# Pooled attention and channel mixing: the two small attention products on quarters of TensorE

## The chip, the core and the metric

The kernel runs on one core of one Trainium2 chip. Its five engines work side by side: TensorE (PE in the profile, with PEld for its weight loads) multiplies matrices, VectorE (DVE), ScalarE (ACT) and GpSimd (POOL) do elementwise work, and SyncE (SP) issues DMAs. The metric is the device time of one execution in microseconds. Before the change it is 623.95 us, the median of three runs from 623.32 to 624.88. A measurement of this kernel can tell about 0.3% from no change.

## The reference

Eight batches, eight heads, 576 tokens, head dimension 64; everything is float32. Keys and values are averaged over groups of eight tokens, so that each head has 72 keys. The attention's output goes through a channel mixing step with a shift by one token.

```python
k_p = k.reshape(B, H, Sp, pool, D).mean(axis=3)          # Sp = 72, pool = 8
v_p = v.reshape(B, H, Sp, pool, D).mean(axis=3)
scores = scale * np.matmul(q, k_p.transpose(0, 1, 3, 2))
attn = np.exp(scores - max); attn = attn / (sum + 1e-09)
x = np.matmul(attn, v_p)                                 # then (B, S, H * D)

x_prev = x shifted by one token within a batch
xk = mu_k * x + (1.0 - mu_k) * x_prev
xr = mu_r * x + (1.0 - mu_r) * x_prev
k = np.maximum(xk @ w_k, 0.0)                            # w_k: 512 x 1024
v = k * k @ w_v                                          # w_v: 1024 x 512
r = 1.0 / (1.0 + np.exp(-(xr @ w_r)))                    # w_r: 512 x 512
out = r * v
```

## The kernel before

The 4608 tokens are cut into 36 tiles of 128 and 12 chunks of 384 tokens (three tiles each). A batch ends every 576 tokens, so four tiles hold tokens of two batches, and four chunks (1, 4, 7, 10) do.

**A tile** goes through `softmax` (line 680). Its scores are four matmuls, one for each pair of heads, at line 700: the queries of 128 tokens are the weights (128 rows: two heads of 64), and the keys of the pair stream by, in a buffer `kbd` in which the two heads' keys stand block by block on a diagonal, the rest zero. So half of the products are with zeros. A tile of two batches needs eight matmuls of 64 columns of weights. Then come the maximum, exponential, sum and reciprocal. The probabilities of 64 of the 72 keys are called the main part, those of the last 8 keys the remainder.

The product with the values needs the probabilities turned, keys by tokens. In chunks 0 and 1 PE turns them (`transposed`, line 815, `transposed_rest`, line 873). From chunk 2 on (`TURNED`) DVE turns blocks of 32 (`turned`, line 773), a DMA takes them to a buffer in DRAM, `passing`, and five DMAs bring a whole chunk back in another order into one buffer `turned_sb` (`fetch_turned`, line 800).

**Precision.** A float32 product can be taken whole, or from numbers that were split in a high and a low part of type fp32r, as three products (high by high, low by high, high by low). Chunk 0 is taken whole, all others are split, both in attention's second product and in the channel mixing. `split_turned` (line 845) splits the probabilities of a tile into `pth` and `ptl`, by an ACT cast and a DVE subtraction over 128 x 512, and makes a third form, `ptr`, for the remainder. The values stand on a diagonal as well: `vbd_h`, `vbd_l` (main) and `vbd_r` (remainder).

**A chunk** goes through `attended` (line 903), once for each pair of heads g = 0..3: four matmuls at line 940 (three main, one remainder; eight in a chunk with two batches) into one PSUM bank of three, then two ACT copies scaled by 1 - mu into `t`, a POOL copy of the token carried from the chunk before, and two DVE operations into `xm`, one for xk and one for xr. `x_parts` (line 978) splits each by an ACT cast and a POOL subtraction (`xkh`, `xkl`, `xrh`, `xrl`). Then `hidden` (line 988, matmuls at line 1011) makes eight tiles of k, each from the four column tiles (ct) of xk, which are the four pairs g; `gate` (line 1045, matmuls at 1063) makes r for three tiles; `mixed` (line 1074, matmuls at 1094) makes the output for three tiles.

**The order** of all instructions is made by a planner when the program is built (class `Order`, line 141). Each of these functions is a thread that says what it needs, what buffer it takes and how long its next step lasts on which engine; the planner gives an engine to the thread that can start first, and of those that could start within 0.1 us to the one with the smallest due time. A table `DUE` overrides due times by name, and other tables say which engine does a sum, a normalisation or a low part (`SUM_BY`, `NORM_BY`, `LOW_BY`, ...) and in which order the inputs are loaded at the start (`LOADS`). Each engine then runs its instructions strictly in the order that the planner wrote.

Of the kernel before, what the change touches and what calls it, by code (L numbers as in the profile page):

```python
# [17 lines left out]
P = 128  # L18
B, H, S, D = 8, 8, 576, 64
POOL = 8  # L20
# [1193 lines left out]
```

## Time and profile before

| | |
|---|---|
| median of the runs | 623.95 us |
| the profiled execution | 625.45 us |
| its span, first to last instruction | 623.6 us |
| mean granted clock of TensorE | 0.997 |
| instructions | 8940 |
| DMA | 68.61 MB, 110 GB/s on average |

The profile gives the busy time of each engine, the span in 40 slices, the chain of work that ended last (followed back from the last instruction, at each step to what released it), and groups of instructions by line. A row of a group reads: line, engine, operation, output <- inputs, shapes, count, then busy time in us and mean ns of one, then the idle time of the engine just before them and what ended it. On PE the mean ns of one matmul holds its way through the array too, and the next one starts earlier; what a stream of them costs is seen in the chain or in the rows in order of time, which show start, duration, line and count. A float32 matmul that isn't split is two records on PE and two weight loads on PEld.

### The profile page before, as it was taken

The numbers are of one execution on the slowest core, as the hardware profiler recorded it, in microseconds if no ns is written. First come the engines' busy times: TensorE is split into PE (matmuls) and PEld (weight loads), VectorE is DVE, ScalarE is ACT, GpSimd is POOL, SyncE is SP. The second block draws the span as 40 slices with busy tenths as digits, with TensorE's granted clock in tenths as the row PEclk, the third lists the DMA queues.
The fourth block names the chain that finished last, engine by engine and source line by source line (L and its number), as shares of the span: only waits on it lengthen the run. The fifth ranks groups of instructions, "written<-read, shape, count | busy, mean of one in ns | idle before, by whom it ended". The sixth has DMA issues, their size and how long they took to land.

```text
span 623.6 us, 8940 instructions
## 1 busy us (share of the span) xinstructions
PE 607.1 (97%) x3100; PEld 524.1 (84%) x3100; DVE 403.0 (65%) x826; ACT 363.7 (58%) x761; POOL 203.4 (33%) x292
## 2 busy tenths in 40 slices
PE   7789999999999999999999999999999999999997
PEld 6755457988988988988988988988988988988986
DVE  4789977975995844884884853794774753623511
ACT  4879975854575744774754753774654643633420
POOL 1130276326415215515614204713713313303100
PEclk9999999999899999999999999999999999999999
DMA  8997221562377132057147124049114013000001
GB/s 263 383 354 239 67 80 62 188 152 70 89 222 186 37 87 77 18 175 193 35 175 176 35 77 105 18 140 227 35 55 112 18 41 88 18 0 35 17 1 51
DMA packets 59453, 68.61 MB, mean 110 GB/s; under 512 B 11664, under 2 KB 43664, under 8 KB 59408
## 3 DMA queue, kind: packets, MB, share of 16 engines
q1 hardware_dynamic: 59264, 67.91, 36.6%
q8 instruction: 24, 0.39, 0.3%
q14 instruction: 21, 0.17, 0.1%
q10 hardware_dynamic: 144, 0.13, 0.1%
HBM read 49.75 MB, written 18.28 MB: 109 GB/s over the span
## 4 chain that ended last, share of the span: by engine, by line
PE 87%; DMA 5%; DVE 3%; POOL 2%; ACT 1%; issue 1%; SPq 0%; DVEq 0%; ACTq 0%; POOLq 0%
PE mm L1094 31%; PE mm L1011 29%; PE mm L1063 15%; PE bank L940 5%; PE sc L700 5%; DMA early_xrl<-in_vm 2%; DMA got_wk<-in_w_k 2%; DMA early_sl<-in_kT 1%; POOL xkl L984 1%; PE bank L448 1%; ACT t L946 1%; PE mm L591 1%; DVE xm L966 1%; POOL xrl L984 0%; ACT xkh L982 0%
## 5 line engine op out<-in xcount | busy, mean ns | idle before, releaser
L1011 PE MATMUL mm<-xkh,w_k 128*128 128x384 f32 x704 | 181.8, 339 | 1.5 <-ACT xkh L982 1.5
L1094 PE MATMUL mm<-w_v,sh 128*128 128x512 f32 x528 | 169.4, 391 | 0.0
L1011 PEld LDWEIGHTS mm<-xkh,w_k 128*128 128x128 f32 x704 | 127.1, 189 | 2.9 <-ACT xkh L982 1.7
L1011 PE MATMUL mm<-xkl,w_k 128*128 128x384 f32 x352 | 118.9, 338 | 1.7 <-POOL xkl L984 1.7
L1094 PEld LDWEIGHTS mm<-w_v,sh 128*128 128x128 f32 x528 | 99.2, 188 | 19.6
L1094 PE MATMUL mm<-w_v,sl 128*128 128x512 f32 x264 | 102.9, 390 | 0.0
L946 ACT ACTIVATE t<-bank,om_sb 128x384 f32<-128x384 f32 x96 | 49.8, 580 | 80.0 <-PE bank L940 78.7
L751 POOL TENSOR_TENSOR e<-e,sm 128x576 f32<-128x576 f32 x30 | 35.6, 1188 | 177.5 <-DVE sm L746 177.5
L1063 PE MATMUL mm<-w_r,xrh 128*128 128x512 f32 x264 | 84.2, 393 | 0.0
L1107 DVE TENSOR_TENSOR rs<-mm,rs 128x512 f32<-128x512 f32 (+1 forms) x37 | 24.9, 675 | 90.6 <-PE mm L1094 90.6
L966 DVE SCALAR_TENSOR_TENSOR xm<-bank,mu_sb,t 128x384 f32<-128x384 f32 x88 | 51.0, 611 | 36.9 <-POOL t L957 17.1
L1037 ACT CAST sh<-rk 128x384 fp32r<-128x384 f32 x88 | 44.8, 514 | 49.7 <-DVE rk L1031 49.4
L1011 PEld LDWEIGHTS mm<-xkl,w_k 128*128 128x128 f32 x352 | 66.6, 189 | 3.2 <-POOL xkl L984 3.2
L984 POOL TENSOR_TENSOR xkl<-xm,xkh 128x384 fp32r<-128x384 f32 x44 | 45.2, 1027 | 70.3 <-ACT xkh L982 70.1
L1039 DVE TENSOR_TENSOR sl<-rk,sh 128x384 fp32r<-128x384 f32 x88 | 51.8, 597 | 12.2 <-ACT sh L1037 10.5
L1063 PEld LDWEIGHTS mm<-w_r,xrh 128*128 128x128 f32 x264 | 49.6, 188 | 10.1
L1094 PEld LDWEIGHTS mm<-w_v,sl 128*128 128x128 f32 x264 | 49.6, 188 | 9.2
L1031 DVE SCALAR_TENSOR_TENSOR rk<-mm,rk 128x384 f32<-128x384 f32 x88 | 47.3, 548 | 11.1 <-ACT rk L1024 10.7
L1063 PE MATMUL mm<-w_r,xrl 128*128 128x512 f32 x132 | 51.4, 389 | 0.0
L1024 ACT ACTIVATE rk<-mm 128x384 f32<-128x384 f32 x88 | 42.2, 487 | 10.8 <-PE mm L1011 7.4
L984 POOL TENSOR_TENSOR xrl<-xm,xrh 128x384 fp32r<-128x384 f32 x44 | 45.6, 1036 | 3.3 <-ACT xrh L982 3.3
L580 POOL TENSOR_TENSOR stage<-stage 128x512 f32<-128x512 f32 (+5 forms) x51 | 45.0, 897 | 1.2
(126 smaller groups left out, 904.2 us busy)
## 6 DMA issues: line engine op xcount, KB each, us to landing
out<-rs SPq DMA_DIRECT2D x35, 256.0 KB, 2.0
passing<-pm SPq DMA_DIRECT2D x30, 288.0 KB, 2.2
qs<-in_qT SPq DMA_DIRECT2D x32, 256.0 KB, 3.6
stage<-in_kT SPq DMA_DIRECT2D x14, 576.0 KB, 4.7
turned_sb<-passing SPq DMA_DIRECT2D x40, 192.0 KB, 4.3
stage<-in_vm SPq DMA_DIRECT2D x14, 512.0 KB, 6.5
got_wk<-in_w_k SPq DMA_DIRECT2D x8, 512.0 KB, 9.0
got_wv<-in_w_v SPq DMA_DIRECT2D x8, 512.0 KB, 11.2
```

The lines of the kernel that those rows point to most:

```text
L580: nc_eng.tensor_tensor(out=st[:, :, :w], in0=st[:, :, :w], in1=st[:, :, w:2 * w], op=ALU.add)
L751: eng.tensor_tensor(out=e, in0=e, in1=sm.broadcast_to([P, 2, 4, KEYS]), op=ALU.mult)
L946: nc.scalar.activation(out=t[:, m, 1:n + 1], in_=xp, func=AF.Copy, scale=om_sb[:, m, g:g + 1])
L966: nc.vector.scalar_tensor_tensor(out=xm[:, :n], in0=xp, scalar=mu_sb[:, m, g:g + 1], in1=t[:, m, :n], op0=ALU.mult, op1=ALU.add,)
L984: nc.gpsimd.tensor_tensor(out=lo, in0=xm[:, :n], in1=hi, op=ALU.subtract)
L1011: nc.tensor.matmul(out=hp, lhsT=w[:, o], rhs=x[:, ct, o_t], start=(ct == 0 and k == 0), stop=(ct == NCT - 1 and k == len(terms) - 1),)
L1024: nc.scalar.activation(out=rk[:, :n], in_=hp, func=AF.Relu)
L1031: nc.vector.scalar_tensor_tensor(out=rk[:, :n], in0=hp, scalar=0.0, in1=rk[:, :n], op0=ALU.max, op1=ALU.mult)
L1037: nc.scalar.copy(out=sh, in_=rk[:, :n])
L1039: nc.vector.tensor_tensor(out=operand("sl", c)[:, jt, o_t], in0=rk[:, :n], in1=sh, op=ALU.subtract)
L1063: nc.tensor.matmul(out=bank, lhsT=x[:, ct, o], rhs=w, start=(ct == 0 and k == 0), stop=(ct == NCT - 1 and k == len(terms) - 1),)
L1094: nc.tensor.matmul(out=bank, lhsT=s[:, o], rhs=w, start=(jt == 0 and k == 0), stop=(jt == NJT - 1 and k == len(terms) - 1),)
```

## The change

Both small attention products are laid on quarters of TensorE: 64 rows (one head's dimension or keys) by 64 columns.

- **Scores** (line 664 of the changed kernel). For each pair of heads, two halves of the tile's tokens (columns) and two heads (rows) make four matmuls with 64 x 64 weights and 72 streamed columns, whole float32: 16 in a tile, whether it holds one batch or two. The two heads write to different banks. The keys stand in `ks` without zeros.
- **Second product** (`attended`, lines 870 and 885). One call now takes two pairs of heads (a = 0, 1) and two PSUM banks at once. First the remainders, as before, with fp32r and 128 columns; then for each batch four matmuls with 64 x 64 weights and up to 384 streamed columns, whole float32, on top of the remainders. What follows the matmuls (`t`, `xm`) is now a thread of its own, `shifted`, one for each bank.
- **Probabilities.** The main part isn't split any more. From chunk 2 on the matmuls read it where the DMA put it, in runs of 32 tokens. `split_turned` makes only `ptr`, once for a chunk. There are two buffers for the turned probabilities, `turned0` and `turned1`, given back after the chunk's second product; early on the second one also serves as room for inputs.
- **Values** stand in `vs` without zeros and unsplit. The buffers `kbd`, `vbd_h`, `vbd_l` and their clearing are gone; keys and values are copied by one ACT instruction and not two.
- The order of channels in `mu`, `w_k` and `w_r` is permuted on the host to suit.
- All the planner's tables and constants are new.

```diff
-LOADS = ("k0 k1 q0 wr3 q2 q1 r0 c0 q3 wk0 wv6 k2 wk1 q5 v1 wk4 wv1 k3 wr2 v0 wr0 wk3 q4 ...")
+LOADS = ("k0 k1 q0 wr3 q1 wv6 r0 c0 q2 q3 v1 wk1 wk4 k2 wk0 q5 k3 wv1 v0 wr2 wk6 wk2 v3 ...")
...
-    "keys 0 0": -9.94, "values 0 0": 24.5, "keys 0 1": -129.19, "values 0 1": -72.82,
+    "keys 0 0": 74.89, "values 0 0": -12.91, "keys 0 1": -160.77, "values 0 1": -59.65,
...
-    kbd = [const.tile([P, NPAIR, 2 * KEYS], F32, name=f"kbd{i}") for i in range(2)]
-    vbd_h = [const.tile([P, NPAIR, P], F32R, name=f"vbd_h{i}") for i in range(2)]
-    vbd_l = [const.tile([P, NPAIR, P], F32R, name=f"vbd_l{i}") for i in range(2)]
+    ks = [const.tile([P, NPAIR, KEYS], F32, name=f"ks{i}") for i in range(2)]
+    vs = [const.tile([P, NPAIR, D], F32, name=f"vs{i}") for i in range(2)]
...
-    turned_sb = const.tile([P, CH // BLOCK, 6 * BLOCK], F32, name="turned_sb")
+    turned_sb = [const.tile([P, CH // BLOCK, 6 * BLOCK], F32, name=f"turned{i}") for i in range(2)]
...
         for g in range(NPAIR):
-            k = (g % 2) * 2 * KEYS
-            for b, _, n, o in parts:
-                nc.tensor.matmul(
-                    out=halves[g // 2][o:o + n, 0, k:k + 2 * KEYS],
-                    lhsT=qs[:, g, o:o + n], rhs=kbd[b % 2][:, g, :], start=True, stop=True,
-                )
+            for o, b in sorted(owner.items()):
+                for h2 in range(2):
+                    r = slice(h2 * D, (h2 + 1) * D)
+                    nc.tensor.matmul(
+                        out=halves[h2][o:o + D, 0, g * KEYS:(g + 1) * KEYS],
+                        lhsT=qs[r, g, o:o + D], rhs=ks[b % 2][r, g, :], start=True, stop=True,
+                    )
...
-    def split_turned(i):
+    def split_turned(c):
...
-        nc.scalar.copy(out=pt_h, in_=main)
-        yield act(2 * P)
         nc.scalar.copy(out=ptr[:rows], in_=rest)
-        yield dve(NPAIR * P)
-        nc.vector.tensor_tensor(out=pt_l, in0=main, in1=pt_h, op=ALU.subtract)
...
-    def attended(c, g, p):
+    def attended(c, a, p):
...
-        bank = yield take("bank")
+        both = [(yield take("bank")), (yield take("bank"))]
...
-                terms = [(vh, ph), (vl, ph), (vh, pl)]
-            terms.append((vbd_r[i][:, r, 2 * j:2 * j + 2, :], operand("ptr", c)[:, r, o]))
-            for q, (v, pt) in enumerate(terms):
-                nc.tensor.matmul(
-                    out=xp[:, to], lhsT=v, rhs=pt, start=(q == 0), stop=(q == len(terms) - 1)
-                )
+        for q, (b, s, k, at) in enumerate(segs):
+            for h2 in range(2):
+                nc.tensor.matmul(
+                    out=both[h2][:, at:at + k], lhsT=vbd_r[b % 2][:, a, 2 * h2:2 * h2 + 2, :],
+                    rhs=operand("ptr", c)[:, a, off + at:off + at + k], start=(q == 0), stop=False,
+                    skip_group_check=True,
+                )
+        for q, (b, s, k, at) in enumerate(segs):
+            for j in range(2):
+                for h2 in range(2):
+                    r, to = slice(h2 * D, (h2 + 1) * D), both[h2][j * D:(j + 1) * D, at:at + k]
+                    if c >= TURNED:
+                        of = (off + at) // BLOCK
+                        pt = held["turned", c][r, of:of + k // BLOCK, (2 * a + j) * BLOCK:(2 * a + j + 1) * BLOCK]
+                        to = to.rearrange("p (a j) -> p a j", j=BLOCK)
+                    else:
+                        pt = operand("pt", c)[r, 2 * a + j, off + at:off + at + k]
+                    nc.tensor.matmul(
+                        out=to, lhsT=vs[b % 2][r, 2 * a + j, :], rhs=pt, start=False, stop=True,
+                        skip_group_check=True,
+                    )
...
+        for h2 in range(2):
+            order.add(att_due[c] + 2 * a + h2, shifted(c, 2 * a + h2, p, both[h2]))
```

What stands in order on PE, at three places. First the scores of a tile between the gate and the mixed products of chunk 2; before:

```order
L1063 MATMUL mm_119<-w_r_655,xrl_1208 128x512
L1063 MATMUL mm_119<-w_r_655,xrh_1207 128x512
L700 MATMUL sc_114<-kbd_70,qs_105 128x144 x4
L1094 MATMUL mm_120<-w_v_1042,sh_1333 128x512
L1094 MATMUL mm_120<-w_v_1042,sl_1373 128x512
```

and now:

```order
L1022 MATMUL mm_117<-w_r_752,xrl_1332 128x512
L1022 MATMUL mm_117<-w_r_752,xrh_1331 128x512
L664 MATMUL sc_112<-ks_70,qs_104 64x72 x16
L1053 MATMUL mm_118<-w_v_1101,sh_1393 128x512
L1053 MATMUL mm_118<-w_v_1101,sl_1450 128x512
```

The place is the same; four matmuls of 144 columns have become sixteen of 72.

Second, the product of chunk 5 between the mixed products of chunk 4, before (one pair of heads at each `L940` group, banks 117 and 115; a few mixed products between):

```order
L1094 MATMUL mm_119<-w_v_1013,sh_2171 128x512
L940 MATMUL bank_117<-pth_2121,vbd_h_72 128x384
L940 MATMUL bank_117<-pth_2121,vbd_l_74 128x384
L940 MATMUL bank_117<-ptl_2122,vbd_h_72 128x384
L940 MATMUL bank_117<-ptr_2123,vbd_r_76 128x384
L1094 MATMUL mm_120<-w_v_1042,sh_2171 128x512
L1094 MATMUL mm_120<-w_v_1042,sl_2211 128x512
L1094 MATMUL mm_120<-w_v_1042,sh_2171 128x512
L940 MATMUL bank_115<-pth_2121,vbd_h_72 128x384
L940 MATMUL bank_115<-pth_2121,vbd_l_74 128x384
L940 MATMUL bank_115<-ptl_2122,vbd_h_72 128x384
L940 MATMUL bank_115<-ptr_2123,vbd_r_76 128x384
```

and now, the second of its two calls:

```order
L1053 MATMUL mm_117<-w_v_1018,sh_2317 128x512
L870 MATMUL bank_115<-ptr_2222,vbd_r_74 128x384
L870 MATMUL bank_114<-ptr_2222,vbd_r_74 128x384
L885 MATMUL bank_115<-turned_98,vs_72 64x384
L885 MATMUL bank_114<-turned_98,vs_72 64x384
L885 MATMUL bank_115<-turned_98,vs_72 64x384
L885 MATMUL bank_114<-turned_98,vs_72 64x384
L1053 MATMUL mm_116<-w_v_1101,sh_2317 128x512
```

Eight matmuls of two pairs of heads have become two remainders and four quarters in one place. From chunk 3 on the two calls of a chunk stand behind the first and the second mixed tile of 24 matmuls, so that a whole mixed tile, and up to chunk 9 a tile's scores too, follow the second call ahead of `hidden`.

Third, the seam from the product of chunk 2 to `hidden` of chunk 2. Before, behind the last pair of heads:

```order
L940 MATMUL bank_116<-ptr_1030,vbd_r_76 128x384
L700 MATMUL sc_114<-kbd_69,qs_107 128x144 x4
L1011 MATMUL mm_120<-xkh_1198,w_k_477 128x384 x2
L1011 MATMUL mm_120<-xkl_1199,w_k_477 128x384
L1011 MATMUL mm_120<-xkh_1198,w_k_477 128x384 x2
L1011 MATMUL mm_120<-xkl_1199,w_k_477 128x384
L1011 MATMUL mm_118<-xkh_1198,w_k_643 128x384 x2
```

and now, behind the second call:

```order
L885 MATMUL bank_115<-turned_99,vs_72 64x384
L970 MATMUL mm_117<-xkh_1316,w_k_507 128x384 x2
L970 MATMUL mm_117<-xkl_1317,w_k_507 128x384
L970 MATMUL mm_117<-xkh_1316,w_k_507 128x384 x2
L970 MATMUL mm_117<-xkl_1317,w_k_507 128x384
L970 MATMUL mm_117<-xkh_1316,w_k_507 128x384 x2
L970 MATMUL mm_117<-xkl_1317,w_k_507 128x384
```

Each x2 and the row behind it are one column tile. Before, a tile's scores stood between, and after two column tiles the next bank's first ones followed; now the first bank's four column tiles follow at once, the third and fourth of which come from the call just ahead. The DMA queue of SP has 186 rows before and now, in another order.

More of the change, by code (lines that the diff above doesn't have):

```diff
@@ L370, in attention_then_channel_mix @@
     early = {}
-    for tag, n in (("sl", 2), ("ptl", 1), ("xrl", 1)):
-        t = sb.tile([P, n, 2 * POOL * KEYS], F32, name=f"early_{tag}", tag=tag)
-        for i in range(n):
+    places = [(tag, sb.tile([P, n, 2 * POOL * KEYS], F32, name=f"early_{tag}", tag=tag)) for tag, n in (("sl", 2), ("xrl", 1))]
+    places.append(("turned", turned_sb[1].rearrange("p a n -> p (a n)").rearrange("p (i n) -> p i n", i=2)))
+    for tag, t in places:
+        for i in range(t.shape[1]):
             got = t[:, i]
@@ L427, in constants @@
         order.make("ident")
-        for b in range(2):
-            yield "pool" if b else "dve", 0.6, False
-            (nc.gpsimd if b else nc.vector).memset(kbd[b], 0.0)
-            order.make(("kbd clear", b))
-        yield "dve", 0.5, False
-        nc.vector.memset(vbd_w, 0.0)
-        order.make(("values clear", 0))
-        for t in (vbd_h[1], vbd_l[1]):
-            yield "pool", 0.5, False
-            nc.gpsimd.memset(t.bitcast(F32), 0.0)
-        order.make(("values clear", 1))
     def warm():
@@ L609, in keys @@
     def keys(b, p):
-        yield need(("k", 2 * b + p), *([("scored", last_tile[b - 2])] if b > 1 else [("kbd clear", b)]))
+        yield need(("k", 2 * b + p), *([("scored", last_tile[b - 2])] if b > 1 else []))
         kind, raw, o = yield from sums(held.pop(("k", 2 * b + p)), KEYS, SUM_BY.get(f"k{2 * b + p}", "v"))
         gs = slice(2 * p, 2 * p + 2)
-        yield "act", 0.53, False
-        for h2 in range(2):
-            r = slice(h2 * D, (h2 + 1) * D)
-            nc.scalar.copy(out=kbd[b % 2][r, gs, h2 * KEYS:(h2 + 1) * KEYS], in_=o[r])
+        yield act(2 * KEYS)
+        nc.scalar.copy(out=ks[b % 2][:, gs], in_=o)
         done_with(kind, raw)
@@ L620, in values @@
     def values(b, p):
-        i = b % 2
-        as_is = b == 0 and whole(0, "p")
-        yield need(("v", 2 * b + p), ("attended", last_chunk[b - 2]) if b > 1 else ("values clear", b))
+        yield need(("v", 2 * b + p), *([("attended", last_chunk[b - 2])] if b > 1 else []))
         if not b:
@@ L626, in values @@
         kind, raw, o = yield from sums(held.pop(("v", 2 * b + p)), D, SUM_BY.get(f"v{2 * b + p}", "g"))
[L627 to L638 removed]
+        yield act(2 * D)
+        nc.scalar.copy(out=vs[b % 2][:, 2 * p:2 * p + 2], in_=o)
         done_with(kind, raw)
         order.make(("values", b, p))
[L641 to L652 removed]
     def last_values(b):
@@ L777, in turned @@
         yield "dve", 0.9, False
-        pairs = e.rearrange("p a (h two) k -> p (a h) two k", two=2)
         for h2 in range(2):
@@ L797, in free_turned, with free_second @@
         yield need(*[("full", kind, i) for kind, n in (("k", NJT), ("r", NCT), ("v", NJT)) for i in range(n)])
-        order.give("turned", turned_sb)
+        order.give("turned", turned_sb[0])
+    def free_second():
+        yield need(("early", "turned", 0), ("early", "turned", 1))
+        order.give("turned", turned_sb[1])
     def fetch_turned(c):
@@ L818, in transposed @@
         yield need(("pm", i), *([("attended", c - 1)] if c else []))
-        if not whole(c, "p"):
-            yield need(("early", "ptl", 0))
         got, pm = held.pop(("pm", i))
@@ L901, in transposed_rest @@
             order.make(("side", first + j))
-    def attended(c, g, p):
+    def attended(c, a, p):
         off, n = parts[c][p]
         segs = stretches(starts[c] + off, n)
-        as_is = whole(c, "p")
         mine = [i for i, t in enumerate(tiles) if t[0] == c and off <= t[1] < off + n]
-        yield need(*[(k, i) for i in mine for k in ("main", "side")])
-        yield need(
-            "om", *[("rest", b) for b, *_ in segs],
-            *[("values" if as_is else "value parts", b, q) for b, *_ in segs for q in range(2)],
-        )
+        if c >= TURNED:
+            yield need(("split", c))
+        else:
+            yield need(*[(k, i) for i in mine for k in ("main", "side")])
+        yield need("om", *[("rest", b) for b, *_ in segs], *[("values", b, a) for b, *_ in segs])
         if c:
@@ L917, in attended @@
             yield need(("early", "xrl", 0))
-        if g:
-            yield need(("attending", c, g - 1, p))
+        if a:
+            yield need(("attending", c, a - 1, p))
         if p:
-            yield need(("shifting", c, g, p - 1))
-        bank = yield take("bank")
+            yield need(*[("shifting", c, 2 * a + h2, p - 1) for h2 in range(2)])
+        both = [(yield take("bank")), (yield take("bank"))]
+        order.make(("attending", c, a, p))
+        yield "pe", SWITCH + sum(2 * pe(k)[1] + pe(k, True)[1] for _, _, k, _ in segs), False
@@ L923, in attended, with shifted @@
+        if c >= TURNED:
+            held["attended", c] = held.get(("attended", c), 0) + 1
+            if held["attended", c] == 2 * len(parts[c]):
+                order.give("turned", held.pop(("turned", c)))
+        order.count(("attended", c), 2 * len(parts[c]))
+        for h2 in range(2):
+            order.add(att_due[c] + 2 * a + h2, shifted(c, 2 * a + h2, p, both[h2]))
+    def shifted(c, g, p, bank):
+        off, n = parts[c][p]
+        segs = stretches(starts[c] + off, n)
         t = yield take("t")
-        order.make(("attending", c, g, p))
@@ L943, in attended @@
-        order.count(("attended", c), NPAIR * len(parts[c]))
         yield "act", 2 * (act(n)[1] + 0.05), False
```

154 lines of the change are left out of this document (53 added, 101 removed), and 112 rows, old and new, of the table DUE.

## The prediction

> **What bounds the kernel now.** First the page: busy times, slices, and the chain of work that ended last.
>
> ```profile
> PE 607.1 (97%) x3100; PEld 524.1 (84%) x3100; DVE 403.0 (65%) x826; ACT 363.7 (58%) x761; POOL 203.4 (33%) x292
> PE   7789999999999999999999999999999999999997
> PEclk9999999999899999999999999999999999999999
> GB/s 263 383 354 239 67 80 62 188 152 70 89 222 186 37 87 77 18 175 193 35 175 176 35 77 105 18 140 227 35 55 112 18 41 88 18 0 35 17 1 51
> PE 87%; DMA 5%; DVE 3%; POOL 2%; ACT 1%; issue 1%; SPq 0%; DVEq 0%; ACTq 0%; POOLq 0%
> ```
>
> PE is busy 97% of the span, carries 87% of the chain, and its clock is full in all slices but one. Work taken off PE is time; work taken off DVE (65%) or ACT (58%) is not. Busy durations overlap on PE, so I take costs from the chain over two chunks, where each piece is the time by which PE advances.
>
> ```profile
> 335.79 1.41 PE bank L940 x8
> 343.36 0.98 PE sc L700 x8
> 344.34 16.81 PE mm L1011 x96
> 362.13 8.20 PE mm L1063 x36
> 371.32 5.45 PE mm L1094 x24
> 383.14 1.77 PE bank L940 x16
> ```
>
> A whole float32 matmul is two records. One tile's scores (four matmuls, eight records) cost 0.98 us, 0.1225 each, and the next piece starts at 343.36 + 0.98 = 344.34: nothing is lost at the seam. The second product for two pairs of heads costs 1.41 (0.176 each), or 1.77 where a batch ends in the chunk (16 of 0.11). Hidden's matmuls take 16.81/96 = 0.175. The hidden, gate and mixed products are untouched.
>
> How often, from the groups by shape:
>
> ```profile
> L700 PE MATMUL sc<-kbd,qs 128*128 128x144 f32 x248 | 36.0, 288 | 1.8 <-ACT e L724 1.1 <-ACT kbd L616 0.6
> L700 PE MATMUL sc<-kbd,qs 128*64 128x144 f32 x64 | 4.8, 292 | 0.0
> L700 PE MATMUL mm<-kbd,qs 128*128 128x144 f32 x8 | 1.2, 299 | 1.7 <-DMA qs<-in_qT 1.7
> L940 PE MATMUL bank<-pth,vbd_h 128*128 128x192 f32 x32 | 9.8, 306 | 0.0
> L940 PE MATMUL bank<-pth,vbd_h 128*128 128x384 f32 x28 | 9.5, 339 | 0.0
> L940 PE MATMUL bank<-pth,rs 128*128 128x384 f32 x8 | 3.3, 499 | 0.6 <-ACT rs L631 0.6
> ```
>
> That is (248 + 8)/8 = 32 tiles of one batch, 64/16 = 4 tiles of two batches, 28/4 = 7 whole chunks, 32/8 = 4 divided ones (1, 4, 7, 10), and chunk 0.
>
> **What the trace shows of parts of TensorE.** The four two-batch tiles already use halves: 64 columns of weights, two outputs. The rows of PE in order of time around one of them, first in a wide and then in a very narrow window:
>
> ```profile
> 163.87 0.34 PE L1011 MATMUL mm<-xkl,w_k 128*128 128x384 f32 x1
> 164.14 1.20 PE L700 MATMUL sc<-kbd,qs 128*64 128x144 f32 x16
> 165.27 0.61 PE L1011 MATMUL mm<-xkh,w_k 128*128 128x384 f32 x2
> 165.71 0.34 PE L1011 MATMUL mm<-xkl,w_k 128*128 128x384 f32 x1
> ```
>
> ```profile
> 164.13 0.20 PEld L700 LDWEIGHTS sc<-kbd,qs 128*64 128x64 f32 x4 [0.25 <-issue]
> 164.14 0.34 PE L700 MATMUL sc<-kbd,qs 128*64 128x144 f32 x2
> ```
>
> Two matmuls start together and last 0.34 as a pair, so halves side by side do run at once: 16 records make eight slots of 0.1225. But the detour is not free. From 163.87 to 165.71 are 1.84 us, of which three whole matmuls are 0.525 and eight slots 0.98; **0.34 us is the price of going to parts and back** (rounded from 0.335).
>
> ```profile
> 55.84 5.81 PE mm L1011 x18
> L700 PEld LDWEIGHTS sc<-kbd,qs x312: 132/190/192, 8.7 to 504.1; 128*128 128x128 f32 x124, 128*64 128x64 f32 x32
> L591 PE MATMUL mm<-early_ptl,ident 128*128 128x144 f32 x16 | 2.2, 292 | 0.6 <-DMA early_ptl<-in_kT 0.6
> ```
>
> A whole float32 record of 384 columns takes 5.81/18 = 0.323, of 144 columns 0.1225: slots follow the columns streamed, so 72 columns should take 0.061. A weight load of 64 columns lasts 132 ns, of 128 columns 190; whole loads follow each other in 0.11 (the 192-column row above), so I put the floor for 64 at 0.11 - 0.058 = 0.052, under 0.061.
>
> **The change, part by part.**
>
> *Scores.* Sixteen quarter matmuls of 72 columns are 32 records, four at once: eight slots of 0.061 = 0.49, plus 0.34 for the detour = 0.83. A one-batch tile gains 0.98 - 0.83 = 0.15, times 32 = 4.8. A two-batch tile pays the detour already: 0.98 + 0.34 - 0.83 = 0.49, times 4 = 2.0.
>
> *Second product, for two pairs of heads.* Whole chunk: two remainder matmuls 0.35, two slots of 0.323 = 0.65, detour 0.34: 1.34 against 1.41, gain 0.07, times 14 = 1.0. Divided chunk: four of 0.11 = 0.44, four slots of 192 columns = 0.65, detour 0.34: 1.43 against 1.77, gain 0.34, times 8 = 2.7. Chunk 0: 4 x 0.323 + 2 x 0.176 = 1.64 against 1.34, times 2 = 0.6.
>
> Sum on PE: 4.8 + 2.0 + 1.0 + 2.7 + 0.6 = **11.1 us**. The uncertain price is the detour, paid 60 times (36 tiles, 24 products). Its ends: nothing (whole float32 next to whole matmuls, as at 343.36) and 0.45 (a third more, for four parts instead of two); the sum is then 31 or 4.5. I take 0.34, the only row of a detour. Reading probabilities in runs of 32 from DMA's buffer I price at nothing: the L591 sums stream two separate runs and last 292 against 288. Its other end, one more slot per product, would cost 24 x 0.32 = 7.7.
>
> *Off PE.* Splitting the probabilities goes (30 casts at 0.62 on ACT, as many subtractions on DVE), as do the zeroed buffers and half of the copies of keys and values. In steady chunks this lay beside PE: nothing. The remainder's split becomes three wide instructions per chunk, with a whole chunk's time before its product, since a second buffer lets DMA land early; the same 186 rows stand in the DMA queue.
>
> ```profile
> L857 ACT CAST pth<-turned_sb 128x512 fp32r<-128x512 f32 x30 | 17.5, 620 | 3.0 <-DMA turned_sb<-passing 3.0
> L946 ACT ACTIVATE t<-bank,om_sb 128x384 f32<-128x384 f32 x96 | 49.8, 580 | 80.0 <-PE bank L940 78.7
> L966 DVE SCALAR_TENSOR_TENSOR xm<-bank,mu_sb,t 128x384 f32<-128x384 f32 x88 | 51.0, 611 | 36.9 <-POOL t L957 17.1
> L982 ACT CAST xkh<-xm 128x384 fp32r<-128x384 f32 x44 | 22.6, 514 | 24.4 <-DVE xm L966 23.9
> L984 POOL TENSOR_TENSOR xkl<-xm,xkh 128x384 fp32r<-128x384 f32 x44 | 45.2, 1027 | 70.3 <-ACT xkh L982 70.1
> ```
>
> *The added wait.* A product now takes two of three banks at once. Behind it on PE stand mixed's matmuls. The second product needs one bank back from the first: two t's (1.16), two xm's (1.22) and a short POOL copy, about 2.6 us, under one 24-matmul mixed tile of 5.45. Hidden.
>
> *The seam to hidden.* After the second product, hidden's third column tile needs xkl of the third pair: four t's 2.32, cast 0.51, POOL 1.03, with latencies about 4.1 us; the fourth 5.1. In steady chunks a mixed tile (5.45), a tile's scores and two column tiles (1.05) stand between: covered. At chunk 2 only 1.05 does, so PE waits about 3.2 us. Before, that seam cost the following, along with a slowed clock, and two later seams also waited:
>
> ```profile
> PE mm L1011 <- POOL xkl L984: 1.7, 3, 0.7
> PE mm L1011 <- ACT xkh L982: 1.5, 1, 1.5
> 150.00:200.00 50.00, 48.06 (x248) 42.86 (x247) 39.16 (x84) 28.28 (x58) 21.81 (x29) 0.97 0.57 155
> 535.51 1.36 POOL xkl L984
> 580.21 1.01 POOL xkl L984
> ```
>
> 3.2 us of waiting is seen, some 2 of it at chunk 2 (the rest at the two last seams, where now a mixed tile covers). So chunk 2 loses 1.2 and the late seams win about 1.2: zero net. The clock (0.97 over 50 us, 1.5 us) I leave as it is.
>
> *Opening.*
>
> ```profile
> 11.92 7.18 DMA early_sl<-in_kT
> 19.12 11.09 DMA early_xrl<-in_vm
> 30.23 10.47 DMA got_wk<-in_w_k
> ```
>
> The first product waits for values that land at 30.23. One 512 KB weight block fewer now stands ahead of them: at 354 GB/s some 1.5 us. I count 1.0, with 3 either way, as every other load also moved.
>
> Sum: 11.1 + 1.0 = 12.1. The profiled execution took 625.45 us (span 623.6), 1.5 above the median of 623.95; 625.45 - 12.1 = 613.3, on the median's scale **611.9**.
>
> **Two rules of the Trainium skill, against the rows.** The pairs' slots keep 0.1225 though each needs a fresh load of 64 columns, so loads hide behind matmuls in the same rows. The Trainium skill, "TensorE: Matmul & The Clock Gate", Part 3 "The mechanism", says that a weight load overlaps running matmuls only where the row group differs. By that rule the slots there would be 0.1225 + 0.058; the trace disagrees.
>
> Sixteen matmuls of that tile start within 0.92 us, 0.057 apiece, by pairs at one moment. The same page of the Trainium skill, Part 1 "Wait — 56ns, not 53.3ns?", gives about 62 ns of sequencer time per matmul when hardware decoding is off. By that figure 32 records need 1.98 and the time would be an estimated 665.
>
> **Rivals.**
> - *Row halves take turns* (slower). Every pair in the trace splits columns; none splits rows. Then scores take 16 x 0.061 + 0.34 = 1.32, +0.34 x 32 = +10.9, two-batch tiles the same; products +0.65 each x 24 - 4.3 = +11.3. With -1.0: 645. It decides once a quarter slot exceeds (0.98 - 0.34)/8 = 0.08.
> - *The sequencer can't feed them* (slower). At 0.057 per record a tile takes 1.82 + 0.34 = 2.16: +1.18 x 32 + 0.84 x 4 - 4.3 - 1.0 = +36, 660. For it: no row shows more than 16 in 0.92; against: pairs start at once. It decides above 0.64/32 = 0.020 per record.
> - *Loads of two quarters follow each other* (slot 0.11): 1.22 per tile, +0.24 x 32 - 0.4 - 4.3 - 1.0 = +2: 626. The 0.1225 slots can't exclude it. Loads not hidden at all (slot 0.119): 1.29, +9.9 - 0.1 + 0.058 x 64 slots - 4.3 - 1.0 = +8: 632.
> - *A cheaper detour* (faster). Shorter slots may leave less to wait for at either seam: at 0.17, 60 x 0.17 = 10 more, 602.
>
> **Chances.** Forecast (604 to 619: opening, runs of 32, the seam) 0.64; cheaper detour 0.12; loads in turn 0.09, not hidden 0.02; row halves 0.07; sequencer 0.06. From 600 to 627 about 0.8 is held: the first three. Measurement separates 0.3%, 1.9 us: faster 0.78 (forecast, detour, a part of loads), within 0.05 (loads), slower 0.17.
>
> **What would show it.** In the chain, a tile's scores at 0.83 with 32 records, starts in fours; 1.3 means row halves or loads, 2 the sequencer. A pair of products at 1.34 and 1.43, the first whole matmul behind a detour late by a tenth or two. PE waiting once, some 3 us, at chunk 2, and hardly after. If PE shows waits on ACT or POOL at every chunk, the cover was misjudged; if values land after 30 us, the opening was.

## The result, and the profile after

| | before | after |
|---|---|---|
| median | 623.63 us (622.97 to 624.88) | 632.73 us (631.79 to 634.48) |
| ratio, 95% interval | | 1.0147 (1.0119 to 1.0174) |
| profiled execution, its span | 625.45 us, 623.6 us | 634.48 us, 632.7 us |
| mean granted clock | 0.997 | 0.985 |

The change made the kernel 9.1 us slower, where 12 us faster was forecast. First the page of the changed kernel: busy times, the granted clock in 40 slices, and the chain by engine.

```profile
PE 602.6 (95%) x4008; PEld 493.2 (78%) x4008; DVE 368.9 (58%) x743; ACT 328.1 (52%) x658; POOL 199.4 (32%) x286
PEclk9989999997999999999899999999999999999999
PE 80%; POOL 6%; DVE 4%; ACT 4%; DMA 3%; issue 2%; SPq 1%; DVEq 0%; POOLq 0%; ACTq 0%
```

Every engine has less to do than before, and PE's share of the chain fell from 87 to 80%: the end is now set, in places, by POOL, ACT and DVE. And the clock dips in four slices, where before it dipped in one. Now the chain of the changed kernel over one whole and the start of one divided chunk (start, us, engine, line, count).

```profile
318.28 0.66 PE sc L664 x32
318.94 8.38 PE mm L1022 x36
...
327.98 5.71 PE mm L1053 x24
333.69 0.35 PE bank L870 x2
334.04 0.81 PE bank L885 x8
334.85 5.66 PE mm L1053 x24
...
380.25 0.43 PE bank L870 x4
380.68 0.81 PE bank L885 x16
381.49 5.67 PE mm L1053 x24
```

For TensorE this is close to the forecast. A tile's 32 score records take 0.66 us and lengthen the piece behind them by 0.18 (8.38 against 8.20 before) or 0.26 (5.71 against 5.45): 0.84 to 0.92, against a forecast of 0.83. A pair of products takes 0.35 + 0.81 = 1.16 us plus 0.21 behind it (5.66 against 5.45), 1.37 against 1.34; in the divided chunk 0.43 + 0.81 + 0.22 = 1.46 against 1.43. So a quarter excursion costs up to 0.09 us more than forecast, an estimated 2 us over all 60, and most of the loss is elsewhere. The waits of the changed kernel, engine by engine (who, for whom: us in total, times, longest us), show where it is.

```profile
ACT vs L612 <- POOL stage L568: 24.5, 5, 6.2
...
PE mm L970 <- DVE rk L990: 12.0, 6, 2.9
...
PE mm L970 <- ACT xkh L941: 2.2, 1, 2.2
```

The same view of the kernel before has no row of PE for `rk` at all, and for the sums only this:

```profile
ACT vbd_h L631 <- POOL stage L580: 3.7, 2, 3.2
```

So the 12.0 us are new; 11.3 of them fall in chunks 4, 5, 7 and 8 and 0.7 in chunk 1. One of the four chunks, at the start of chunk 5's hidden, in order of time:

```profile
297.61 8.04 POOL L568 TENSOR_TENSOR stage<-stage 128x512 f32<-128x512 f32 x9
302.70 0.72 ACT L612 COPY vs<-stage 128x128 f32<-128x128 f32 x2 [6.24 <-POOL stage L568]
303.15 0.34 PE L970 MATMUL mm<-xkl,w_k 128*128 128x384 f32 x1
...
304.88 0.49 ACT L983 ACTIVATE rk<-mm 128x384 f32<-128x384 f32 x1
305.41 0.56 DVE L990 SCALAR_TENSOR_TENSOR rk<-mm,rk 128x384 f32<-128x384 f32 x1
306.02 0.56 PE L970 MATMUL mm<-xkh,w_k 128*128 128x384 f32 x1 [2.52 <-DVE rk L990]
```

POOL sums the values of a later batch, nine additions in 8.04 us. ACT stands for 6.24 us before the copy of these sums; behind it in its queue are an exponential, a cast and then the first relu of hidden (`rk`, 304.88), whose input, the twelve matmuls of hidden's first tile of k that began at about 297, was ready soon after 299. (The expectations of e2, e3 and e5 call these eight tiles of k hidden's column tiles.) DVE finishes it at 305.97. PE has three banks `mm`, has filled them with three tiles of k by 303.4, and needs the first one back: it stands for 2.52 us. The same is seen in chunks 4, 7 and 8, the chunks behind which the values of batches 4, 6 and 7 are summed. Behind some of these waits the clock drops, and behind two waits for x in chunks 0 and 2 as well, as the windows show (start:end, length, busy us of the five engines with counts, granted clock, DMA share, GB/s):

```profile
30.00:37.00 7.00, 4.86 (x23) 1.91 (x22) 4.78 (x10) 2.92 (x6) 2.05 (x5) 0.76 1.07 376
145.00:160.00 15.00, 12.63 (x57) 11.03 (x56) 5.08 (x9) 7.44 (x16) 12.50 (x16) 0.77 0.34 71
303.00:310.00 7.00, 4.47 (x17) 4.16 (x16) 5.23 (x13) 4.48 (x11) 3.60 (x5) 0.76 0.73 236
451.00:460.00 9.00, 6.13 (x26) 5.81 (x26) 6.33 (x16) 5.51 (x12) 4.49 (x7) 0.81 0.08 33
```

A mean of 0.76 over 7 us is 3.4 us at half speed (7 x 0.24 x 2). The four places hold 3.4, 6.9, 3.4 and 3.4 us, 17.1 in all, half of it lost: 8.5 us. Before there was one such place, in chunk 2 (0.76 over the 7 us from 155, again 3.4 us at half speed, 1.7 lost).

With the forecast's own -11.1 on PE and -1.0 in the opening, +12.0 at `rk` and +6.8 by the clock make +6.7; the last matmul begins 6.6 us later than before (625.9 against 619.4). The two forecast terms in this sum are not measurements, so the agreement is in part luck. The profiled span is longer by 9.1: the last DMA issue on ACT took 2.62 us there and 0.37 before. It took 0.37 again in e1, whose PE order is the same, and 2.14 in e3, so it goes with the execution and not with the change.

### The profile page after: what moved, and what is told of

Same layout as the page of the kernel before. It is cut to its first block, busy times and chain, and to the rows that moved or that the text cites. A ratio compares the mean times of both kernels' runs of the same rounds, so it can differ in the third digit from the quotient of the medians.

```text
span 632.7 us, 10535 instructions
## 1 busy us (share of the span) xinstructions
PE 602.6 (95%) x4008; PEld 493.2 (78%) x4008; DVE 368.9 (58%) x743; ACT 328.1 (52%) x658; POOL 199.4 (32%) x286
## 4 chain that ended last, share of the span: by engine, by line
PE 80%; POOL 6%; DVE 4%; ACT 4%; DMA 3%; issue 2%; SPq 1%; DVEq 0%; POOLq 0%; ACTq 0%
PE mm L970 28%; PE mm L1053 27%; PE mm L1022 16%; POOL stage L568 4%; PE bank L885 3%; PE sc L664 3%; ACT t L905 2%; DMA early_xrl<-in_kT 2%; DMA stage<-in_vr 1%; PE bank L870 1%; POOL xrl L943 1%; DVE stage L568 1%; DVE xm L925 1%; PE mm L579 1%; ACT xkh L941 0%
## 5 line engine op out<-in xcount | busy, mean ns | idle before, releaser
L970 PE MATMUL mm<-xkh,w_k 128*128 128x384 f32 x704 | 185.4, 345 | 14.2 <-DVE rk L990 12.0
L1053 PE MATMUL mm<-w_v,sh 128*128 128x512 f32 x528 | 171.4, 396 | 0.0
L970 PEld LDWEIGHTS mm<-xkh,w_k 128*128 128x128 f32 x704 | 129.8, 193 | 18.3 <-DVE rk L990 13.7
L970 PE MATMUL mm<-xkl,w_k 128*128 128x384 f32 x352 | 120.5, 342 | 0.2 <-POOL xkl L943 0.2
L715 POOL TENSOR_TENSOR e<-e,sm 128x576 f32<-128x576 f32 x29 | 34.1, 1175 | 187.6 <-DVE sm L710 181.3
L905 ACT ACTIVATE t<-bank,om_sb 128x384 f32<-128x384 f32 x96 | 48.2, 584 | 65.7 <-PE bank L885 65.7
L970 PEld LDWEIGHTS mm<-xkl,w_k 128*128 128x128 f32 x352 | 67.9, 193 | 0.9 <-POOL xkl L943 0.9
L990 DVE SCALAR_TENSOR_TENSOR rk<-mm,rk 128x384 f32<-128x384 f32 x88 | 48.6, 552 | 23.3 <-ACT rk L983 23.0
L943 POOL TENSOR_TENSOR xrl<-xm,xrh 128x384 fp32r<-128x384 f32 x44 | 47.5, 1087 | 5.6 <-ACT xrh L941 5.6
L1066 DVE TENSOR_TENSOR rs<-mm,rs 128x512 f32<-128x512 f32 (+1 forms) x37 | 24.7, 670 | 40.7 <-PE mm L1053 40.6
L568 POOL TENSOR_TENSOR stage<-stage 128x512 f32<-128x512 f32 (+5 forms) x48 | 41.6, 889 | 1.3
```

The costliest lines, as they stand in the source:

```text
L568: nc_eng.tensor_tensor(out=st[:, :, :w], in0=st[:, :, :w], in1=st[:, :, w:2 * w], op=ALU.add)
L715: eng.tensor_tensor(out=e, in0=e, in1=sm.broadcast_to([P, 2, 4, KEYS]), op=ALU.mult)
L905: nc.scalar.activation(out=t[:, m, 1:n + 1], in_=xp, func=AF.Copy, scale=om_sb[:, m, g:g + 1])
L943: nc.gpsimd.tensor_tensor(out=lo, in0=xm[:, :n], in1=hi, op=ALU.subtract)
L970: nc.tensor.matmul(out=hp, lhsT=w[:, o], rhs=x[:, ct, o_t], start=(ct == 0 and k == 0), stop=(ct == NCT - 1 and k == len(terms) - 1),)
L990: nc.vector.scalar_tensor_tensor(out=rk[:, :n], in0=hp, scalar=0.0, in1=rk[:, :n], op0=ALU.max, op1=ALU.mult)
```

## The experiments

Behind them is one table, made from PE's rows in order of time: when the first gate matmul of a chunk starts, against the kernel before, in us. It compares one profiled execution of each run; that of the kernel before took 625.45 us, 1.7 to 2.0 above its medians beside the runs (623.47 to 623.77), and those of the changed kernel and of e5 lie 1.8 and 3.0 above their own, so the last column is not the difference of the medians.

| run | median | chunk 0 | 2 | 3 | 5 | 8 | 11 | last matmul |
|---|---|---|---|---|---|---|---|---|
| changed kernel | 632.73 | -1.6 | -2.4 | -0.8 | +4.1 | +10.6 | +6.6 | +6.6 |
| e5, copies and casts later | 620.28 | -0.8 | -1.2 | +0.5 | +0.3 | +1.0 | -2.2 | -2.2 |
| e8, plan mended | 622.93 | -0.8 | +4.8 | +6.0 | +3.7 | +0.2 | -3.0 | -3.0 |
| e9, mended from chunk 3 | 616.92 | -1.9 | -4.1 | +0.6 | -1.8 | -5.3 | -8.5 | -8.5 |
| e10, and seams filled | 615.86 | -2.8 | -5.0 | -0.3 | -2.7 | -6.2 | -9.4 | -9.4 |
| e7, kernel before with new scores | 621.55 | -1.3 | -1.3 | -1.6 | -2.2 | -3.2 | -3.6 | -3.6 |

### Without the copy, and with the copy later (e1, e2): a miss

In e1 the last addition of a sum gets `vs` as its output (the change inside `sums` is left out here); in e2 only a need is added.

```diff
@@ values (e1) @@
-    kind, raw, o = yield from sums(held.pop(("v", 2 * b + p)), D, SUM_BY.get(f"v{2 * b + p}", "g"))
-    yield act(2 * D)
-    nc.scalar.copy(out=vs[b % 2][:, 2 * p:2 * p + 2], in_=o)
+    to = vs[b % 2][:, 2 * p:2 * p + 2]
+    kind, raw, o = yield from sums(held.pop(("v", 2 * b + p)), D, SUM_BY.get(f"v{2 * b + p}", "g"), to if b >= 4 else None)
+    if o is not None:
+        yield act(2 * D)
+        nc.scalar.copy(out=to, in_=o)
@@ values (e2) @@
+    if b >= 4:
+        yield need(("hid", last_chunk[b - 2], 3, 0))
     yield act(2 * D)
     nc.scalar.copy(out=vs[b % 2][:, 2 * p:2 * p + 2], in_=o)
```

> The changed kernel, but for batches 4 to 7 POOL's last addition of each value sum writes straight into vs, so that ACT has no copy of values there; the order of PE's matmuls is the same. Theory (ACT waits 6 us in that copy for POOL's sums, with hidden's first two relu's queued behind it, so that PE waits 2.5 us for a bank in chunks 4, 5, 7 and 8): PE's waits for DVE's rk fall from 12.0 us to under 2, ACT's waits for POOL's sums at that line from 24.5 to under 3, the clock keeps full speed at 306 and 456 us, and the time is 615 to 619 us against 632.7. Rival A (POOL's value sums delay the low parts xkl, or the quarters themselves cost it, and ACT's copy only stands beside): the waits turn into waits for xkl or others, time 628 or more. Rival B (waits go, but the lost time is elsewhere): 624 to 628.

> The changed kernel with all its work, but for batches 4 to 7 ACT's copy of the values is ordered only after hidden's fourth column tile has been issued; the order of PE's matmuls is the same. Theory (only the place of the copy in ACT's order costs the time): within 2 us of the run without the copy, 615 to 620 us, PE's waits for rk under 2 us. Rival (the copy's own work on ACT, or POOL's burst of sums, is what costs): 628 or more.

Measured: 633.01 us (ratio to the kernel before 1.0164, 1.0139 to 1.0188) and 633.46 us (1.0166, 1.0137 to 1.0195). Nothing was won: both theories failed. The waits of e1 and then of e2:

```profile
ACT vq L630 <- POOL stage L568: 19.7, 4, 5.3
...
PE mm L977 <- DVE rk L997: 12.4, 5, 4.1
...
ACT vs L619 <- POOL stage L568: 0.4, 1, 0.4
```

```profile
ACT vq L625 <- POOL stage L568: 19.1, 4, 5.0
...
PE mm L972 <- DVE rk L992: 10.9, 5, 4.1
...
ACT vs L614 <- POOL stage L568: 0.9, 1, 0.9
```

The copies' own wait is gone (24.5 to 0.4 and 0.9), and the next instruction of ACT that needs POOL's sums has taken it over: the cast of the remainder values `vq`, which needs all nine additions and stands behind the first relu and ahead of the second. PE stands as long as before, for the second bank and not the first. By these two runs alone the theory could have been given up; the row of `vq` says it was only too narrow.

### Both later (e5)

```diff
@@ values: as in e2; last_values: @@
+    if b >= 4:
+        yield need(("hid", last_chunk[b - 2], 5, 0))
     vq = yield take("vq")
```

> The changed kernel with all its work; for batches 4 to 7 both the copies of the values (after hidden's fourth column tile) and the cast of the remainder values vq (after its sixth) are ordered later on ACT. The run with the copies alone moved still waited, 12 us at rk, now 5.2 us on ACT in front of the cast of vq, which needs all nine of POOL's sums. Theory (any ACT instruction that needs these sums and stands ahead of hidden's relu's costs the same wait; together they are the loss): PE's waits for rk under 2 us, no half clock behind chunk 3, time 614 to 620 us. Rival A (a third consumer takes the wait over, DVE's steps on the values or the products of the next chunk but one): 626 or more. Rival B (the loss is in the quarters' neighbours): 626 or more, without waits on PE.

Measured: 620.28 us, ratio 0.9952 (0.9935 to 0.9970): 12.4 us less than the changed kernel, by the place of three instructions per batch in ACT's order; one place for a tile's scores moved too, from chunk 4 to chunk 9. The granted clock is full from chunk 3 on. The waits, and two rows of DVE in chunk 4:

```profile
PE mm L974 <- DVE rk L994: 5.6, 5, 1.7
...
ACT vs L614 <- POOL stage L568: 0.4, 1, 0.4
```

```profile
259.62 0.77 DVE L747 STREAM_TRANSPOSE pm<-e 128x256 f32<-128x256 f32 x2 [4.05 <-POOL e L719]
...
260.88 0.55 DVE L994 SCALAR_TENSOR_TENSOR rk<-mm,rk 128x384 f32<-128x384 f32 x1
```

What is left, 5.6 us, is mostly a third form of the same (0.7 of it is again the wait in chunk 1, which no edit touched): POOL normalises a tile's probabilities behind its nine additions, DVE waits 4.05 us for them with its transposes, and `rk` stands behind these in DVE's queue. That is rival A in small; the theory's figure for `rk` (under 2) was missed, its time by 0.3.

### The clock (e3)

```diff
+    if jt == 3 and ct == 0 and c in (4, 5, 7, 8):
+        unused = min(order.slots["bank"], key=lambda h: h[0])[1]
+        for _ in range(10):
+            nc.tensor.matmul(out=unused[:, :P], lhsT=ident, rhs=ident, start=True, stop=True)
```

> The changed kernel with ten matmuls of the identity by itself (128 columns, whole float32, about 2.2 us in all, into a bank that nobody reads) put on PE ahead of hidden's fourth column tile in chunks 4, 5, 7 and 8, where it waits 2.3 to 3.05 us; ACT's order stays. Theory (idle PE of over some 2.4 us costs a stretch of half clock behind it, 3.4 us long in two of the four chunks): the half-speed stretches at 306 and 456 us vanish and the time falls by 3 to 4 us, to 629 to 630; the waits in sum with the filling stay 10 to 12 us. Rival (the half-speed stretches come by themselves or follow something else): no change or up to 2 us slower, 632 to 635.

Measured: 629.75 us, 3.0 less than the changed kernel, ratio 1.0107 (1.0088 to 1.0126). Its windows:

```profile
300.00:315.00 15.00, 14.70 (x92) 14.51 (x91) 10.92 (x26) 7.63 (x17) 5.93 (x9) 1.00 0.55 168
450.00:465.00 15.00, 14.36 (x115) 13.67 (x114) 11.24 (x25) 9.12 (x20) 3.27 (x4) 1.00 0.37 80
```

The two stretches of half clock behind the waits are gone, with the waits still there, only filled with work for nobody. So two of the waits for `rk` cost 1.7 us each more than themselves. The theory's limit of some 2.4 us doesn't hold: waits of 2.09 and 2.19 us were followed by half clock too. The last section shows what decides.

### The sums planned as if they took no time, in the kernel before (e4)

```diff
-    yield (dve if eng == "v" else pool)(2 * n * cols)
+    yield ("pool", 0.0, True) if early else (dve if eng == "v" else pool)(2 * n * cols)
```

(`early` is set for the value sums of batches 4 to 7.)

> The kernel before the change, with one thing of the changed kernel's order: for batches 4 to 7 the planner counts POOL's value sums as taking no time, so that ACT's casts of the values stand ahead of hidden's first or second relu; the order of PE's matmuls and all the work are unchanged. Theory (this order alone costs the time, whatever TensorE's parts do): PE waits for rk at four chunks, 8 to 12 us in all, with one or two stretches of half clock: 632 to 639 us against 623.6. Rival (the order is harmless without the quarters): 623 to 625.

Measured: 648.48 us, ratio 1.0403 (1.0383 to 1.0423), 24.7 us slower: more than expected, and by another path. The edit moved more than ACT's casts. POOL's own order changed, and the waits are for x and not for `rk`; its waits, and POOL, ACT and POOL again in chunk 4:

```profile
PE mm L1011 <- ACT xkh L982: 14.6, 5, 3.9
```

```profile
247.25 5.97 POOL L580 TENSOR_TENSOR stage<-stage 128x512 f32<-128x512 f32 x7
253.17 0.19 POOL L953 COPY t<-carry 128x2 f32<-128x2 f32 x1
254.32 0.51 ACT L982 CAST xkh<-xm 128x384 fp32r<-128x384 f32 x1 [4.22 <-DVE xm L966]
```

The copy of one token, 0.19 us of work, stood behind seven additions, and the last quarter of x with it. The clock has its share: four stretches, 20.5 us at half speed, against one of 3.4 before. So this run doesn't show what it was made for, and the kernel before with ACT's casts alone earlier wasn't tried. It shows that in the kernel before, too, without any quarters, a misjudged place of POOL's sums costs 24.7 us with PE's matmuls in the same order.

### The scores alone (e7)

```diff
-    for b, _, n, o in parts:
-        nc.tensor.matmul(out=halves[g // 2][o:o + n, 0, k:k + 2 * KEYS], lhsT=qs[:, g, o:o + n], rhs=kbd[b % 2][:, g, :])
+    for o, b in sorted(owner.items()):
+        for h2 in range(2):
+            nc.tensor.matmul(out=halves[h2][o:o + D, 0, g * KEYS:(g + 1) * KEYS], lhsT=qs[r, g, o:o + D],
+                             rhs=kbd[b % 2][r, g, h2 * KEYS:(h2 + 1) * KEYS])
...
```

> The kernel before the change with the scores alone on quarters of TensorE (32 records a tile, and the order of heads in e, pm and px that goes with it; keys still read from the zero-padded buffer); the planner's costs are not touched, so every engine keeps its order. Theory (quarters are a plain gain of 0.15 us per one-batch tile and 0.49 per two-batch tile wherever the order is undisturbed): 6.8 us less than 623.8, 616 to 618 us, with no new waits. Rival (shorter scores only move the waits elsewhere, for the engines beside PE have no room): 621 to 624.

Measured: 621.55 us, ratio 0.9969 (0.9959 to 0.9979), a gain of 2.0 where 6.8 was expected. Its chain in steady chunks:

```profile
358.67 0.66 PE sc L702 x32
359.33 8.38 PE mm L1065 x36
...
368.38 5.71 PE mm L1096 x24
```

PE's order is the same as before but for the scores, so the two traces can be laid side by side matmul by matmul. A tile of one batch gains 0.14 to 0.15 us, as forecast, where hidden follows it, but only 0.12 to 0.13 where the gate follows and 0.07 to 0.08 where mixed follows: 0.34 for the three tiles of a chunk where 0.45 was forecast. The two tiles of two batches behind chunk 3 gain 0.47 each (0.49 forecast) and lose it at once, for x isn't ready earlier: in chunks 5 and 8 PE now waits 0.43 and 0.42 us for `xkl`, where before it didn't.

```profile
PE mm L1013 <- POOL xkl L986: 2.0, 4, 0.7
```

That is how the table comes to -3.6 at chunk 9 from -1.6 at chunk 3, 2.0 where the forecast's prices give 3.4. At chunk 2 the gain stands still; PE waits 2.9 us there for `xkh`, against 1.5 before. So the scores win on their own, but less than was forecast, and a tuned order gives part of it back at its tight seams. Theory and rival each hold in part; the time is the rival's.

### The plan (e8, e9)

Why did the copies come to stand there? Each follow-up of a second product, `shifted`, is a thread of its own in the changed kernel. In the kernel before it was the same thread as the product, and so was planned after it. The new thread asks only for a buffer `t`: nothing tells the planner that the product must be done. In the planner's own times the `t` of chunk 5's second product start at 268.3 and the product ends at 272.4 us. On the chip nothing can go wrong by that, since the engines' semaphores hold; but the plan believes that x and POOL's sums are ready 4 us early, and writes ACT's queue accordingly.

```diff
@@ attended, behind the matmuls @@
+    order.make(("product", c, a, p))
@@ shifted, ahead of its first step (in e9 for c >= 3 only) @@
+    yield need(("product", c, g // 2, p))
```

> The changed kernel with one line more in its planner: the thread that follows a second product (shifted) is planned no earlier than the end of that product's matmuls, as it was in the kernel before, where both were one thread. In the changed kernel's plan the t of the second product of chunk 5 starts at 268.3 and the product itself ends at 272.4, so x's low parts and POOL's value sums are planned some 4 us too early. Work is the same; every engine's order is planned anew (chunks 0 to 2 most). Theory (this lost need is why ACT's copies stand ahead of the relu's): in chunks 4, 5, 7 and 8 the cast vq comes behind two relu's, PE's waits for rk fall from 12 us to under 3, time 612 to 621. Rival (the new order brings other waits in chunks 0 to 2, where banks are short): rk's waits are gone and the time is still 622 to 632. Rival (the plan's times are not what sets the copies' place): rk's waits stay, 630 or more.

> The changed kernel with the planner's lost need put back from chunk 3 on only, so that chunks 0 to 2 keep the changed kernel's order, in which the mended plan lost 6 us. Against the kernel before, the first gate matmul of chunk 3 then comes 0 to 2 us earlier, as in the changed kernel, and from there to the end PE gains what the mended plan gained there (from +6.0 us at chunk 3 to -3.0 at the end, 9 us). Theory (TensorE's gain was real, and only the lost need in steady chunks and the seam at chunk 2 hid it): 612 to 616 us. Rival (the mended plan's gain behind chunk 3 was only a catching up of what it had lost in chunk 2): 619 to 622.

Measured: e8 622.93 us, ratio 0.9987 (0.9976 to 0.9998); e9 616.92 us, ratio 0.9897 (0.9881 to 0.9913). e8's first rival held: from chunk 3 on it gains 9 us, but its new order of chunks 0 to 2 loses 6 (10.2 us at half clock in chunk 2, against 3.4 before, are 3.4 of it). e9, whose order on PE is the changed kernel's up to chunk 3, has both: 15.8 us less than the changed kernel for three lines that add no work, 0.9 above what was expected. From there on e9 also puts the scores of a few tiles elsewhere, so e5 is the narrower test of ACT's order. Waits of e9, and POOL and ACT in chunk 5:

```profile
PE mm L973 <- DVE rk L993: 0.7, 1, 0.7
```

```profile
288.79 3.25 POOL L568 TENSOR_TENSOR stage<-stage 128x512 f32<-128x512 f32 x2
292.24 0.74 POOL L568 TENSOR_TENSOR stage<-stage 128x256 f32<-128x256 f32 x1
293.44 1.02 POOL L946 TENSOR_TENSOR xkl<-xm,xkh 128x384 fp32r<-128x384 f32 x1 [0.47 <-ACT xkh L944]
297.75 4.38 POOL L568 TENSOR_TENSOR stage<-stage 128x256 f32<-128x256 f32 x6
297.83 0.49 ACT L986 ACTIVATE rk<-mm 128x384 f32<-128x384 f32 x1
298.94 0.72 ACT L612 COPY vs<-stage 128x128 f32<-128x128 f32 x2 [0.62 <-POOL stage L568]
```

With a true plan POOL does three of the nine additions while it waits for x (288.79 to 293), the first relu stands ahead of the copies, and ACT waits 0.62 us where it waited 6.24.

### And the two seams left (e10)

```diff
+    if jt == 0 and (c, ct) in ((0, 0), (2, 2)):
+        unused = min(order.slots["bank" if c else "mm"], key=lambda h: h[0])[1]
+        for _ in range(8 if c == 0 else 10):
+            nc.tensor.matmul(out=unused[:, :P], lhsT=ident, rhs=ident, start=True, stop=True)
```

> As the run mended from chunk 3 on, with matmuls of the identity by itself (whole float32, into banks that nobody reads) where PE waits in the two seams left: eight ahead of hidden's first matmul in chunk 0 (1.8 us, where it waits 2.25) and ten ahead of hidden's third column tile in chunk 2 (2.2 us, where it waits 2.36). Theory (each of these waits is followed by a stretch of half clock, 3.4 us or 6.8 long): the stretches at about 34 and 150 us vanish, 3 to 5 us less than that run, 608 to 612. Rival (the clock at those places falls anyway, because PE is thinly used there over several us): within 1.5 us of that run.

Measured: 615.86 us, ratio 0.9879 (0.9865 to 0.9892). The clock in 40 slices:

```profile
PEclk9999999999999999999999999999999999999999
```

Both stretches are gone, so the rival's reason fell; but the time is 1.1 us below e9, within the rival's 1.5 and not the theory's 3 to 5. With only two single stretches left in e9 (0.93 over 25 us and 0.89 over 15 us, 3.5 and 3.3 us at half speed), 3.4 was the most to be had, and the filling takes a part. This is the fastest version of the study, 7.6 us below the kernel before.

## Why the prediction was wrong, step by step

- **What bounds the kernel** (PE, and its clock): right.
- **Scores, second product, detour, runs of 32**: right in kind, a little too cheap. The detour cost 0.34 to 0.43, by what follows it (e7 shows the tiles, the chain the products with 0.37), where 0.34 was taken for all from one row of the kernel before, with hidden behind it; the rivals on TensorE that made it slower (row halves, sequencer, weight loads) fell with the rows of 0.66 us for 32 records. So did the two rules of the Trainium skill, "TensorE: Matmul & The Clock Gate", Part 3 "The mechanism" and Part 1 "Wait — 56ns, not 53.3ns?": the first would have given 0.12 a slot, the second 1.98 us a tile; whether its condition, hardware decoding off, is met here no run shows. From chunk 3's gate to the last matmul e9 gains 9.1 us. Three tiles more lie ahead of that point than before, worth 2.9 (3 x 0.98); PE's waits behind it are 0.5 shorter (1.2 before, 0.7 in e9); the other 5.7 are, in sum, what the forecast's prices give (13 tiles of 0.15, two of 0.49, ten whole products of 0.07, six divided of 0.34). That they fit so well is in part luck, since e7's tiles gained less.
- **Opening**: forecast -1.0, within 3 either way. The first product starts 3.3 us earlier (29.66 against 32.95), so the term was too small. At chunk 0's gate 1.6 are left: a wait for x in chunk 0 had 3.4 us of half clock behind it, 1.7 lost, which the forecast hadn't.
- **The added wait (two banks)** and **the seam to hidden in steady chunks**: "Hidden" and "covered" held. No wait for `xkl` or for a bank of the second product stands in the changed kernel's steady chunks; PE's stops are for `rk`.
- **The seam at chunk 2**: 3.2 us forecast, 2.2 seen. The half clock behind it was 6.9 us in the changed kernel's profile, 3.4 lost, but 3.4 us in e1, e3 and e9 with the same order on PE up to there, as long as before. So "The clock (...) I leave as it is" held there but for the execution; it failed in chunk 0 and behind `rk`.
- **"Off PE. (...) In steady chunks this lay beside PE: nothing" is the step that failed.** It counted which work went and found ACT and DVE lighter. It didn't ask in which order the work that stayed would stand in each queue. The forecast followed the product's path to x and its banks, but not POOL's value sums and what of ACT stands behind them, though the order of the changed kernel shows two copies and a cast around hidden's first relu, where the kernel before had two relu's ahead. In place of nothing the runs showed 11.3 us of waiting at `rk` in chunks 4, 5, 7 and 8, and with the half clock behind two of these waits 14.7. e2 and e5 together show the place on ACT to be the cause; e9 shows the lost need in the plan to be behind it. With that need put back the kernel takes 616.92 us, still 5.0 above the forecast of 611.9: the half clock in chunk 0 is 1.7 of it, and the rest is open.
- **The rivals and the chances**: 0.17 for slower lay wholly on TensorE's mechanisms. None lay on the planner, which the change had rewritten. The prediction's last sentence but one did name the sign: PE's waits for ACT at many chunks mean that the cover was misjudged.

## What to carry to other kernels

Where a planner writes the order, a change of its threads is a change to the program: when one thread is cut in two, see that the second still needs what the first makes, or the plan runs ahead of the chip. Before engines with low busy shares are priced at nothing, go through each queue that runs strictly in order and look for an instruction that waits for a slow engine's burst ahead of one that feeds the bottleneck. If taking away a suspected wait changes nothing, read who waits now: a second instruction with the same need may stand right behind.

## What the runs showed of the hardware

- The clock of TensorE drops to half behind waits of little over 2 us, but not behind each. Two matmuls that end such waits in the changed kernel, and the stretches around each wait:

```profile
33.27 1.01 PE L970 MATMUL mm<-xkh,got_wk 128*128 128x384 f32 x1 [2.09 <-DVE xkh L925]
256.57 0.45 PE L970 MATMUL mm<-xkh,w_k 128*128 128x384 f32 x1 [2.13 <-DVE rk L990]
```

```profile
29.71:33.12 3.41, 1.42 (x12) 0.44 (x11) 2.46 (x5) 2.41 (x6) 0.22 (x2) 1.00 1.11 347
33.12:36.53 3.41, 3.26 (x12) 1.49 (x12) 2.61 (x6) 0.78 (x2) 1.83 (x3) 0.50 1.03 406
254.99:258.40 3.41, 1.83 (x10) 1.83 (x11) 2.21 (x6) 2.71 (x7) 2.91 (x4) 1.00 0.88 318
258.40:261.81 3.41, 3.41 (x22) 3.30 (x21) 3.35 (x10) 1.78 (x4) 0.00 (x0) 1.00 0.46 169
```

  What decides is where the wait falls. In each of the eleven traces, the changes of the granted clock lie whole multiples of 3.413 us apart (in the changed kernel half clock begins at 33.12, and then 34, 80 and 124 such steps later), which makes a fixed row of windows. The wait of 2.09 us fell almost wholly into one window and left PE busy for 1.42 us of it: the next window has half clock. The wait of 2.13 us was cut by an edge, PE was busy for 1.83 us in the window that holds most of it, and the clock stayed full. Over all traces there are 1941 windows at full clock. In 29 of them PE stood idle for 1.82 us or more, and half clock followed each; in the other 1912 it stood for 1.80 us or less, and half clock followed none. Why a stretch lasts one window or two isn't shown. The Trainium skill, "TensorE: Matmul & The Clock Gate", Part 1 "What's actually happening", gives a free-running window of about 3.4 us and a drop after at least one idle window. The windows agree; but a window that was idle for little over half of its length was enough here.
- Filling a wait with matmuls that nobody reads kept the clock full (e3 and e10), for 3.0 and 1.1 us.
- Four quarters of TensorE ran side by side with a new 64 x 64 weight load for each matmul: 32 records of 72 columns in 0.66 us. The excursion from whole matmuls to quarters and back cost 0.34 to 0.43 us, for the 32 records of a tile's scores as for the 8 or 16 of a product (0.37).
